# Attention and feed-forward on one core: two block loads moved ahead of waiting copies on GpSimd, and a new order of steps

## The chip, the core and the metric

The kernel runs on one core of a Trainium2 chip. Its engines are TensorE (PE, matrix products; PEld is its weight load), VectorE (DVE), ScalarE (ACT), GpSimd (POOL) and SyncE (SP, which only issues transfers). Each engine works through its own queue in order; semaphores make one engine wait for another. DMA transfers are issued from the queues of SP, ACT and POOL. The metric is the device time of one execution in microseconds (us); lower is better.

## What is computed

Sliding-window causal attention over 8 batch entries, 8 heads, 576 positions, 64 values per head, then a feed-forward layer over all 4608 tokens:

```python
scores = scale * np.matmul(q, k.transpose(0, 1, 3, 2))
rel = pos[:, None] - pos[None, :]
mask = (rel >= 0) & (rel < 64)
scores = np.where(mask, scores, -1000000000.0)
attn = np.exp(scores - max); attn = attn / attn.sum
x = (attn @ v).transpose(0, 2, 1, 3).reshape(4608, 512)
h = x @ w_in                                  # 512 x 2048
out = (h * sigmoid(1.702 * h)) @ w_out        # 2048 x 512
```

All arrays are float32 outside; the kernel computes products in bfloat16.

## The kernel before, in words

**Attention.** Tokens are taken in 36 groups m of 128, that is two query blocks of 64; a batch entry has nine such blocks, so a group can span two entries. A query block j needs the keys of positions 64(j-1) to 64(j+1). Keys and queries must stand transposed (`qt`, `kt`, two sets used in turn by even and odd entries). `scores(m)` (L319) multiplies them into the bank pair psS, `exp` (L335) runs on ACT, `mask` (L339) multiplies by the band on VectorE, `pv` or `pv_two` (L347) multiplies by the values (from `v_nat` for odd j, from `v_off`, the same values shifted by 64 rows, for even j), `norm` or `norm_two` (L363, L365, L391, L392) divides on VectorE, and the result is transposed into `xT`, up to m = 15 by TensorE and an ACT copy (`x_mm`, L415, L424, L434, L431), from m = 16 by a transposing DMA on SP (`x_dma`, L437).

**How rows arrive.** Entries 0 and 1 are loaded in float32 and cast. Of entry 2, the third one, blocks 0 to 2 (128 rows each) are loaded in float32 by SP (`load_qk` L108, `load_v` L87) and cast by GpSimd: the queries and keys of block 2 by the copies L969 and L972, the values by `cast_v` (L101), in three pieces. From block 3 of entry 2 on, `load_bf16(b, i)` (L228, L229) issues three transfers from the GpSimd queue (queries, keys, values) that convert on the way. `turn_dma(b, i)` (L240) then transposes the queries and keys of a block by two DMAs from the SP queue, and `shift_v` (L233, L235) makes the shifted values on GpSimd.

**Feed-forward.** A unit s of `w_in` work is eight or sixteen products into one of two banks psH (`up_mm`, L453), 0.87 us on TensorE. It ends either in one ACT operation (`up_gelu`, L484) or in a tanh on ACT (`up_th`, L464) and a multiplication on VectorE (`up_g`, L479); either frees the bank. Sixteen units make the 512 tokens of a chunk. The product with `w_out` and, for the last chunk, the one with `w_in` are done with seven block products in place of eight (Strassen's way): sums of blocks of g are formed on VectorE (`add_g`, L544), differences of weight blocks once (`add_w`, L528), and the products p1 to p7 (`product`, L568) of each 256 tokens go in two bank chains of psO, which has two banks. `keep_chain` copies a chain's state out in the middle (L113), `add_out` (L593) and `last_of_chain` (L113) write the output tile `o_sb`, of which there are five, and `store` (L584) sends it off, from SP or ACT.

**What sets the order.** The program runs under a manual schedule: every engine executes in the order in which the program issues. Up to L1020 the order is written out as calls. After it a string `plan` holds 727 steps, executed one by one. A step is a letter with numbers:

- `u`s`.g` or `u`s`.t`: unit s, with gelu on ACT, or with tanh and a later `g`s on VectorE
- `c`m scores (`.h`: in two psH banks), `x`m exp (with a load of the ACT table where the last operation was gelu), `m`m mask, `v`m the product with the values, `n`m norm, `t`m transposition
- `l`b.i `load_bf16`, `y`b.i `turn_dma`, `h`b.i `shift_v`
- `p`q.n product n of the 256 tokens q, `a`q.n a sum of g, `w`n.part a difference of weights, `k`q.n.E `keep_chain` on engine E, `o`q.n `add_out`, `z`q.E `last_of_chain`, `s`q.t `store`
- `F K O G X W`: the same for the last chunk's product with `w_in`

As each engine's queue is in order, a step's place in the plan fixes what stands ahead of it on its engine, but an engine runs ahead of the others until it has to wait.

Of the kernel before, what the change touches and what calls it, by code (L numbers as in the profile page):

```python
# [29 lines left out]
def kernel(  # L30
# [39 lines left out]
    def size(i):  # L70
        return P if i < 4 else 64
# [627 lines left out]
    def warm(n):  # L699
# [270 lines left out]
    load_v(2, 2)  # L970
    cast_v(2, 1, parts=(0,))
    nc.gpsimd.tensor_copy(out=rows[0][1][0:size(2), 2, :], in_=stage_of_qk(2, 2)[0:size(2), 1, 0:DM])  # L972
# [15 lines left out]
    load_bf16(2, 3)  # L988
# [20 lines left out]
    load_bf16(2, 4)  # L1009
# [15 lines left out]
        u32.t g32 u33.t g33 l3.0 c10 x10 m10 l3.1 y2.3 v9 h2.3 h2.4 y3.0 h3.0 p2.1 u34.t y2.4 l3.2  # L1025
        c11 n9 x11 g34 u35.t m11 g35 t9 p2.2 v10 w3.0 u36.g n10 l3.3 u37.t g37 u38.g t10 u39.g u40.g
        u41.g u42.g u43.g u44.g u45.g w1.1 u46.g w2.1 l3.4 a2.3 a2.1 w1.0 a2.2 a2.4 h3.1 y3.1 k2.1.V
        w3.1 w2.0 o2.2 a3.3 p2.6 p2.5 h3.2 a3.1 k2.6.V p2.7 k2.7.A w4.1 w4.0 l4.0 y3.2 u47.g y3.3
        a3.2 a3.4 c12 x12 p2.4 o2.5 p2.3 z2.V p3.1 o2.3 h3.3 k3.1.V m12 p3.2 o3.2 h3.4 c13 x13 p3.6
        k3.6.A p3.5 p3.7 m13 y3.4 k3.7.V o3.5 v12 c14 p3.4 z3.A x14 n12 p3.3 t12 p4.1 c15 x15 y4.0  # L1030
        a4.3 a4.1 a4.2 o3.3 a4.4 u48.t u49.g p4.2 u50.g g48 l4.1 y4.1 u51.g u52.g u53.g k4.1.V o4.2
        m15 s2.0 s3.0 m14 c16 x16 v14 n14 m16 c17.h x17 l4.2 p4.5 p4.6 k4.6.V t14 m17 u54.g p4.7 v16
        n16 c18 l4.3 t16 h4.0 l4.4 u55.g u56.g u57.g u58.g k4.7.V o4.5 u59.t g59 u60.g p4.3 o4.3
        a5.3 h4.1 a5.1 s3.1 l5.0 y4.2 h4.2 p4.4 z4.V x18 p5.1 h5.0 l5.3 l5.2 k5.1.A u61.t a5.2 h4.3
        h4.4 y4.3 p5.2 c19 g61 y4.4 p5.6 x19 u62.g u63.g m18 k5.6.V p5.7 k5.7.A m19 v18 o5.2 u64.g
        n18 u65.g l5.1 y5.0 u66.g u67.g h5.1 h5.2 u68.g u69.g p5.5 c20 x20 a5.4 c21.h x21 s4.0 p5.4
# [24 lines left out]
        O33.3 a16.3.0 G33.3 F34.2 p14.2 O34.2 G34.2 K35.1.V u127.g p14.4 o14.2 F35.6 K35.6.A F35.2
        F34.6 K34.6.A a16.1.0 a15.3 F34.5 F35.7 O35.2 G35.2 s12.0 a15.1 p14.5 a16.2.0 z14.A o14.5
# [116 lines left out]
```

The softmax here doesn't subtract the row's maximum and nothing guards it: scores larger than these inputs give would overflow.

## Time and profile before

Six runs gave 293.54 to 300.89 us, median 296.1. The profiled execution took 296.88 us; its span, from the first to the last recorded instruction, was 295.2 us, so 1.7 us lie around it.

| from the profile | us |
| --- | --- |
| profiled execution, own time | 296.88 |
| its span | 295.2 |
| last product of TensorE ends | 291.88 |
| ACT table loads after 70 us, 21 | 26.9 |
| GpSimd issues of `load_bf16`, 81 | 69.8 |
| landing of `kt` transposes, shortest / median / longest | 2.3 / 5.9 / 8.8 |
| landing of `xT` transposes | 2.4 / 5.2 / 8.4 |
| landing of a 256 KB output store from SP, from ACT (median) | 4.2, 2.1 |
| granted TensorE clock | 0.998 |

How to read it: a row of the timeline has start, duration, engine, line, operation, output and inputs, and in brackets the time that the engine stood idle before and what ended that wait. The releaser is inferred and can name the wrong one of several. Matmul ends are modelled, and products overlap slightly, so consecutive products start 0.87 us apart though one row says 1.04. Of the DMA rows, the duration is that of issuing alone; landing comes later.

### The profile page before, as it was taken

What the parts mean: (1) busy time and instruction counts of PE and PEld (TensorE: products, weight loads), DVE (VectorE), ACT (ScalarE), POOL (GpSimd) and SP (SyncE); (2) the same over time, 40 slices, a digit from 0 to 9 for tenths busy, and PEclk for the clock granted to TensorE, in tenths of its full rate; (3) what the DMA queues carried; (4) which work ended last, traced back from release to release, by engine and by line L of the source; (5) the groups of instructions that cost most, each with busy time, mean ns of one, the idle gap of its engine ahead of it and who ended that gap; (6) DMA issues with size and microseconds to landing.
All of it is one profiled execution on the core that took longest, in us unless ns stands there. A gap on an engine that the chain in (4) does not pass through costs nothing.

```text
span 295.2 us, 8971 instructions
## 1 busy us (share of the span) xinstructions
PE 283.9 (96%) x3778; PEld 250.9 (85%) x3783; DVE 196.7 (67%) x377; ACT 181.1 (61%) x289; POOL 137.6 (47%) x191
## 2 busy tenths in 40 slices
PE   8699999999999989999999999999999999999995
PEld 8478455999898878889898999899899899989984
DVE  4667725898998685375546663775887874768771
ACT  3577535877774388776768665776758653456411
POOL 1580446744999989706829876209640000000000
PEclk9999999999999999999999999999999999999999
DMA  7999999996999999999999999999975171001133
GB/s 233 215 205 215 243 240 234 252 153 127 86 132 108 138 145 139 177 169 132 130 184 125 153 137 215 150 179 165 157 82 126 26 192 39 0 2 71 73 124 126
DMA packets 149768, 42.79 MB, mean 145 GB/s; under 512 B 135136, under 2 KB 144864, under 8 KB 149728
## 3 DMA queue, kind: packets, MB, share of 16 engines
q0 software_dynamic: 77712, 13.64, 67.2%
q1 hardware_dynamic: 68208, 25.18, 50.3%
q10 hardware_dynamic: 3808, 3.41, 3.7%
q8 instruction: 29, 0.48, 0.7%
q14 instruction: 11, 0.09, 0.1%
HBM read 36.70 MB, written 9.44 MB: 156 GB/s over the span
## 4 chain that ended last, share of the span: by engine, by line
PE 78%; DMA 9%; POOL 5%; DVE 3%; issue 2%; ACT 2%; SPq 0%; ACTq 0%; DVEq 0%
PE hps L453 32%; PE chain L568 16%; PE part L568 13%; PE ops L491 5%; PE up L668 4%; PE Tacc L347 3%; DMA kt<-rows_k 3%; DMA stage_qk<-in_k_dram 3%; DMA out_dram<-o_sb 3%; PE S L319 3%; POOL v_off L101 2%; DVE stage_qk L528 1%; POOL v_nat L101 1%; POOL w_in_sb L247 1%; PE turn L196 1%
## 5 line engine op out<-in xcount | busy, mean ns | idle before, releaser
L453 PEld LDWEIGHTS <-w_in_sb 128*128 128x128 bf16 x1312 | 109.6, 113 | 4.9 <-issue 0.7
L484 ACT ACTIVATE gT<-hps 128x512 bf16<-128x512 f32 x82 | 48.6, 597 | 34.7 <-PE hps L453 34.4
L453 PE MATMUL hps<-xT_pe,w_in_sb 128*128 128x128 bf16 (+2 forms) x800 | 60.9, 234 | 0.1
L453 PE MATMUL hps<-xT_dma,w_in_sb 128*128 128x256 bf16 x512 | 60.6, 273 | 0.3 <-ACT gT L694 0.3
L568 PEld LDWEIGHTS <-gT 128*128 128x128 bf16 x512 | 49.0, 98 | 5.9
L479 DVE SCALAR_TENSOR_TENSOR gT<-th,hps 128x512 bf16<-128x512 bf16 x46 | 30.8, 684 | 12.4 <-ACT th L464 12.3
L233 POOL COPY v_off<-v_nat 64x528 bf16<-64x528 bf16 x27 | 18.7, 695 | 37.4 <-DMA v_nat<-in_v_dram 36.7
L464 ACT ACTIVATE th<-hps 128x512 bf16<-128x512 f32 x46 | 27.0, 599 | 12.9 <-PE hps L453 12.5
L593 DVE TENSOR_TENSOR o_sb<-part,stage_v 128x256 f32<-128x256 f32 x48 | 20.2, 422 | 21.6 <-PE part L568 12.8
L335 ACT ACTIVATE PT<-S 128x1024 bf16<-128x1024 f32 x28 | 28.5, 1017 | 8.6 <-PE S L319 8.3
L339 DVE TENSOR_TENSOR PT<-PT,band_all 128x1024 bf16<-128x1024 bf16 x32 | 23.7, 750 | 5.4 <-ACT PT L335 5.3
L229 POOL DMA_DIRECT2D v_nat<-in_v_dram x27 | 23.4, 866 | 2.3 <-DMA rows_q<-in_q_dram 1.1
L228 POOL DMA_DIRECT2D rows_k<-in_k_dram x27 | 23.3, 863 | 2.3 <-DMA v_nat<-in_v_dram 2.3
L228 POOL DMA_DIRECT2D rows_q<-in_q_dram x27 | 23.1, 854 | 0.0
L568 PEld LDWEIGHTS <-sums 128*128 128x128 bf16 x192 | 18.6, 98 | 3.7 <-issue 1.6
L568 PEld LDWEIGHTS <-stage_v 128*128 128x128 bf16 x192 | 18.6, 98 | 2.1
L113 ACT COPY stage_v<-chain 128x256 f32<-128x256 f32 x22 | 8.2, 373 | 18.8 <-PE chain L568 18.8
L113 DVE COPY stage_v<-chain 128x256 f32<-128x256 f32 x26 | 10.9, 420 | 11.7 <-PE chain L568 11.5
L392 DVE TENSOR_TENSOR xs<-Tacc,rc 128x128 bf16<-128x128 f32 (+1 forms) x26 | 18.0, 692 | 0.9
L568 PE MATMUL chain<-stage_qk,sums 128*128 128x256 bf16 x128 | 16.6, 272 | 0.4 <-DVE stage_v L113 0.4
L319 PEld LDWEIGHTS <-kt 64*128 64x128 bf16 x576 | 10.4, 95 | 7.4 <-issue 5.2
L568 PE MATMUL chain<-stage_qk,gT 128*128 128x256 bf16 x128 | 16.6, 273 | 0.0
(127 smaller groups left out, 458.4 us busy)
## 6 DMA issues: line engine op xcount, KB each, us to landing
out_dram<-o_sb SPq DMA_DIRECT2D x24, 256.0 KB, 4.2
rows_q<-in_q_dram POOLq DMA_DIRECT2D x21, 128.0 KB, 6.9
rows_k<-in_k_dram POOLq DMA_DIRECT2D x21, 128.0 KB, 7.4
v_nat<-in_v_dram POOLq DMA_DIRECT2D x21, 128.0 KB, 8.1
out_dram<-o_sb ACTq DMA_DIRECT2D x10, 256.0 KB, 2.1
stage_v<-in_v_dram SPq DMA_DIRECT2D x9, 256.0 KB, 7.0
stage_qk<-in_q_dram SPq DMA_DIRECT2D x4, 512.0 KB, 7.3
stage_qk<-in_k_dram SPq DMA_DIRECT2D x4, 512.0 KB, 8.0
```

The costliest lines, as they stand in the source:

```text
L113: (nc.scalar.copy if engine is nc.scalar else engine.tensor_copy)(**kw)
L228: nc.gpsimd.dma_start(out=heads(row_block(b, i, w)), in_=rows_of(src, b, i))
L229: nc.gpsimd.dma_start(out=v_nat[b % 2][0 : size(i), i, :, 0:D], in_=rows_of(v, b, i))
L319: nc.tensor.matmul(st[h % 2][:, t * 256 + hp * 64 : t * 256 + hp * 64 + 64], lhsT=src[1][part, hp, 64 * j : 64 * j + 128], rhs=src[0][part ...
L335: nc.scalar.activation(out=e[:], in_=st[:], func=AF.Exp, scale=scale)
L339: nc.vector.tensor_tensor(out=pt, in0=pt, in1=band_all[:], op=ALU.mult)
L453: nc.tensor.matmul(ps[:, g, :], lhsT=w_in[:, c, (f + g) % 4 : 512 : 4], rhs=xT[ch][:, m0 : m0 + nt // P, c, :], start=(c == 0), stop=(c == 3),
L464: nc.scalar.activation(out=th[:], in_=ps[:], func=AF.Tanh, scale=1.702)
L479: nc.vector.scalar_tensor_tensor(out=g_of(*unit), in0=th[:], scalar=1.0, in1=ps[:], op0=ALU.add, op1=ALU.mult,)
L484: nc.scalar.activation(out=g_of(*unit), in_=ps[:], func=AF.Gelu_apprx_sigmoid, scale=2.0)
L568: nc.tensor.matmul(out[:, :], lhsT=left[:, j], rhs=right[:, j], start=new and j == 0, stop=j == 7, skip_group_check=True,)
L593: nc.vector.tensor_tensor(out=out_half(c, pr, t, half), in0=C_of[c, pr][:], in1=kept(c, pr, at), op=ALU.add)
```

## The change

In the part written out as calls, `load_bf16(2, 3)` and `load_bf16(2, 4)` move up. The first now stands between the copies of block 2's queries and of its keys, the second right after the copy of the keys; that copy moves ahead of `cast_v(2, 1, parts=(0,))`. Before, the first stood behind the key copy and four casts, the second behind three casts more.

The plan is replaced by another one of 730 steps. The same products, sums, loads, transposes and stores are in it. Seventeen of its units instead of fourteen are done by tanh and VectorE. In its first part the differences w1 and w2 stand at the front, scores 12 come right after unit 36 and not after unit 47, and the loads of entries 3 and 4 stand earlier. Stores 4.1, 5.0 and 8.1 stand later and store 7.0 earlier. The last steps are in another order: `p16.4` is now the last product instead of `p17.4`.

The diff, the plan cut to its beginning and end:

```diff
@@ -968,8 +968,10 @@
     up_g(*UU['1.12.128'])
     nc.gpsimd.tensor_copy(out=rows[0][0][0:size(2), 2, :], in_=stage_of_qk(2, 2)[0:size(2), 0, 0:DM])
     load_v(2, 2)
+    load_bf16(2, 3)
+    nc.gpsimd.tensor_copy(out=rows[0][1][0:size(2), 2, :], in_=stage_of_qk(2, 2)[0:size(2), 1, 0:DM])
+    load_bf16(2, 4)
     cast_v(2, 1, parts=(0,))
-    nc.gpsimd.tensor_copy(out=rows[0][1][0:size(2), 2, :], in_=stage_of_qk(2, 2)[0:size(2), 1, 0:DM])
     cast_v(2, 2, parts=(0,))
     cast_v(2, 1, parts=(1,))
     cast_v(2, 1, parts=(2,))
@@ -985,7 +987,6 @@
     UU['1.4.256'] = up_th(*UU['1.4.256'])
     cast_v(1, 3, nc.vector, parts=(1,))
     up_g(*UU['1.4.256'])
-    load_bf16(2, 3)
     turn_dma(2, 2)
     UU['1.8.256'] = up_mm(1, 8, 4, 256, 128, wide=True)
     x_mm(7, psT, "T")
@@ -1006,7 +1007,6 @@
     UU['1.4.384'] = up_th(*UU['1.4.384'])
     up_g(*UU['1.12.256'])
     up_g(*UU['1.4.384'])
-    load_bf16(2, 4)
     UU['1.8.384'] = up_mm(1, 8, 4, 384, 128, wide=True)
     UU['1.8.384'] = up_th(*UU['1.8.384'])
     up_g(*UU['1.8.384'])
@@ -1022,51 +1022,51 @@
 
 
     plan = """
-        u32.t g32 u33.t g33 l3.0 c10 x10 m10 l3.1 y2.3 v9 h2.3 h2.4 y3.0 h3.0 p2.1 u34.t y2.4 l3.2
-        c11 n9 x11 g34 u35.t m11 g35 t9 p2.2 v10 w3.0 u36.g n10 l3.3 u37.t g37 u38.g t10 u39.g u40.g
-        u41.g u42.g u43.g u44.g u45.g w1.1 u46.g w2.1 l3.4 a2.3 a2.1 w1.0 a2.2 a2.4 h3.1 y3.1 k2.1.V
-        w3.1 w2.0 o2.2 a3.3 p2.6 p2.5 h3.2 a3.1 k2.6.V p2.7 k2.7.A w4.1 w4.0 l4.0 y3.2 u47.g y3.3
-        a3.2 a3.4 c12 x12 p2.4 o2.5 p2.3 z2.V p3.1 o2.3 h3.3 k3.1.V m12 p3.2 o3.2 h3.4 c13 x13 p3.6
-        k3.6.A p3.5 p3.7 m13 y3.4 k3.7.V o3.5 v12 c14 p3.4 z3.A x14 n12 p3.3 t12 p4.1 c15 x15 y4.0
-        a4.3 a4.1 a4.2 o3.3 a4.4 u48.t u49.g p4.2 u50.g g48 l4.1 y4.1 u51.g u52.g u53.g k4.1.V o4.2
-        m15 s2.0 s3.0 m14 c16 x16 v14 n14 m16 c17.h x17 l4.2 p4.5 p4.6 k4.6.V t14 m17 u54.g p4.7 v16
...
-        p16.5 a17.4.1 o17.2 k16.7.V o16.5 p17.5 s15.1 p16.4 o17.5 s17.1.1 s17.0.0 p17.3 o17.3
-        s17.0.1 z16.A s16.1 p16.3 o16.3 s16.0 p17.4 z17.A s17.1.0
+        u32.t g32 w1.0 w2.0 c10 p2.1 l3.0 l3.1 w1.1 l3.2 x10 v9 y2.3 l3.3 n9 h2.3 h2.4 u33.t g33
+        u34.t g34 y2.4 m10 c11 x11 p2.2 l3.4 y3.0 k2.1.A t9 u35.t m11 u36.t h3.0 c12 g35 h3.1 x12
+        g36 v10 y3.1 n10 l4.1 u37.g u38.t l4.0 t10 u39.g g38 h3.2 y3.2 u40.g u41.g u42.g u43.g w3.0
+        w2.1 u44.g u45.g h3.3 w3.1 u46.g a2.3 y3.3 o2.2 a3.3 a3.1 h3.4 a2.1 a2.2 w4.0 p2.6 k2.6.A
+        p2.5 m12 p2.7 a3.2 w4.1 a2.4 k2.7.V c13 x13 p2.4 o2.5 m13 z2.V p2.3 p3.1 v12 c14 y3.4 k3.1.A
+        a4.3 a4.1 p3.6 k3.6.A o2.3 n12 p3.2 t12 l4.2 p3.7 x14 u47.t u48.t l4.4 a3.4 o3.2 c15 x15
+        h4.0 k3.7.V y4.0 p3.5 p3.4 g47 z3.A m14 m15 y4.1 u49.t g48 a4.2 p4.1 k4.1.V c16 o3.5 v14
+        p4.6 x16 n14 k4.6.A h4.1 c17 x17 p3.3 o3.3 u50.g s3.1 t14 y4.4 l4.3 p4.2 o4.2 p4.7 u51.g
+        p4.5 g49 l5.0 u52.g a4.4 h4.2 k4.7.V p4.4 m17 m16 v16 n16 u53.g c18 s3.0 u54.g l5.2 u55.g
+        u56.g a5.3 u57.g a5.1 u58.g u59.g u60.t o4.5 p4.3 h4.3 h4.4 a5.2 z4.V g60 x18 t16 o4.3 p5.1
+        k5.1.V l5.3 y4.2 s2.1 u61.t h5.0 p5.2 s2.0 p5.6 k5.6.V c19 x19 m18 y4.3 y5.0 g61 o5.2 u62.g
+        p5.7 s4.0 a5.4 a6.3 u63.t p5.5 l5.1 h5.1 u64.g u65.g u66.g u67.g u68.g u69.g g63 c20 l5.4
+        m19 v18 a6.1 y5.2 k5.7.V p5.4 a6.2 a6.4 n18 u70.g u71.g o5.5 z5.V p6.1 k6.1.V l6.0 p5.3 o5.3
+        x20 a7.3 m20 p6.6 k6.6.A p6.2 o6.2 t18 c21 x21 p6.7 h5.2 y5.1 p6.5 h5.3 h5.4 c22 m21 y5.3
+        v20 x22 k6.7.V p6.4 n20 y5.4 u72.g u73.g u74.g t20 a7.1 u75.g u76.g u77.g z6.V y6.0 p7.1
+        a7.2 m22 o6.5 p6.3 o6.3 c23.h k7.1.V x23 c24 x24 h6.0 s5.1 p7.2 p7.6 m23 v22 s6.0 n22 u78.g
+        u79.g u80.g u81.g u82.g u83.g u84.g a7.4 k7.6.V p7.7 t22 l6.1 y6.1 o7.2 p7.5 m24 l6.2 y6.2
+        c25.h x25 h6.1 c26 k7.7.V o7.5 p7.4 x26 z7.A m25 h6.2 u85.g s7.1 p7.3 v24 p8.1 m26 n24 t24
+        s6.1 u86.g u87.g u88.g l7.0 k8.1.V u89.g l6.3 u90.g u91.g u92.g u93.g u94.g l7.1 o7.3 a9.3
+        a9.1 a8.3 y6.3 a8.1 a8.2 u95.g h6.3 p8.6 k8.6.V p8.2 c27.h x27 p8.7 s7.0 a9.2 h7.0 y7.0 o8.2
+        p8.5 k8.7.A l6.4 c28 h6.4 y7.1 x28 c29.h x29 h7.1 a8.4 p8.4 z8.A o8.5 p8.3 m27 v26 o8.3
+        u96.g p9.1 k9.1.A u97.g a9.4 s8.0 n26 p9.6 l7.3 p9.2 l7.2 h7.2 m28 h7.3 l7.4 h7.4 k9.6.A
+        u98.t g98 u99.g p9.7 k9.7.A y6.4 u100.g u101.g a10.3 a10.1 a10.2 p9.4 m29 u102.g u103.g t26
+        z9.V p10.1 a10.4 o9.2 p9.5 k10.1.V p10.6 o9.5 s9.1 y7.2 c30.h x30 k10.6.V m30 c31 p9.3 o9.3
...
+        p15.3 G34.3 a17.3.1 a17.1.1 o15.3 a17.1.0 z15.A p16.1 a17.2.0 s15.1 a17.2.1 a17.4.0 p17.1
+        p17.2 a16.4.0 k16.1.V k17.1.A p17.6 a16.4.1 p16.2 a17.4.1 o16.2 s14.0 k17.6.A o17.2 p17.7
+        s15.0 p16.6 k16.6.V k17.7.A p17.5 p17.4 p16.7 p16.5 z17.V s17.0.0 o17.5 k16.7.V o16.5 p17.3
+        p16.3 s14.1 s17.1.0 p16.4 o16.3 s16.0 o17.3 s17.1.1 z16.A s16.1 s17.0.1
```

## The prediction

> **What bounds the kernel now.** I read first the busy totals, then the busy time of each engine by stretches, then the list of who waited for whom, with TensorE alone.
>
> ```profile
> PE 283.9 (96%) x3778; PEld 250.9 (85%) x3783; DVE 196.7 (67%) x377; ACT 181.1 (61%) x289; POOL 137.6 (47%) x191
> ```
>
> ```profile
> 60.00:80.00 20.00, 19.65 (x420) 18.39 (x418) 18.35 (x34) 15.45 (x26) 11.12 (x17) 1.00 1.04 117
> 80.00:90.00 10.00, 9.93 (x176) 9.80 (x174) 9.32 (x15) 7.06 (x13) 9.84 (x12) 1.00 1.95 128
> 90.00:100.00 10.00, 9.57 (x120) 8.26 (x119) 7.65 (x14) 5.20 (x8) 9.54 (x13) 1.00 1.63 114
> 100.00:110.00 10.00, 8.98 (x135) 7.77 (x134) 7.66 (x16) 5.49 (x8) 8.73 (x11) 1.00 2.46 144
> 120.00:130.00 10.00, 9.14 (x85) 8.65 (x83) 4.89 (x9) 6.74 (x12) 4.56 (x7) 1.00 1.90 191
> 280.00:296.00 16.00, 11.88 (x109) 10.40 (x107) 7.37 (x20) 1.86 (x5) 0.00 (x0) 0.94 0.31 115
> ```
>
> Columns: stretch, length, then busy us of PE, PEld, DVE, ACT, POOL, then the granted clock. TensorE sets the time at full clock. Summed over the stretches from 60 to 280 us it is idle 3.26 us, 2.7 of that in the five stretches shown before the last. The change alters no matmul and nothing that runs before about 66 us. So the most that the reordering can bring there is 3.26 us, 1.1% of 296.9, and only if it adds no wait. What the idle time waited for:
>
> ```profile
> PE S L319 <- DMA kt<-rows_k: 0.9, 1, 0.9
> PE part L568 <- DVE o_sb L593: 0.9, 1, 0.9
> PE chain L568 <- DVE stage_v L113: 0.4, 1, 0.4
> PE Tacc L347 <- POOL v_off L101: 0.3, 1, 0.3
> ```
>
> In order of time: v10 waits 0.35 for a GpSimd cast (78.5 us), p2.7 waits 0.42 for k2.6 on VectorE (92.0), c15 waits 0.94 for the transposed keys of y3.2 (106.5), p4.3 waits 0.85 because o4.5 had no free output buffer until store s2.0 or s3.0 landed (126.0). The first two belong to compute queues, the last two are single late transfers. Short waits of 0.33 and 0.12 lie later.
>
> **Part 1, the GpSimd loads.** The timeline of POOL:
>
> ```profile
> 65.36 0.70 POOL L969 CAST rows_q<-stage_qk 128x512 bf16<-128x512 f32 x1 [2.61 <-DMA stage_qk<-in_q_dram]
> 70.52 0.61 POOL L101 CAST v_off<-stage_v 64x512 bf16<-64x512 f32 x1 [4.47 <-PE pxt L415]
> 71.19 0.61 POOL L972 CAST rows_k<-stage_qk 128x512 bf16<-128x512 f32 x1
> 74.12 0.90 POOL L228 DMA_DIRECT2D rows_q<-in_q_dram  x1
> 78.98 0.70 POOL L228 DMA_DIRECT2D rows_q<-in_q_dram  x1
> 81.01 0.92 POOL L228 DMA_DIRECT2D rows_q<-in_q_dram  x1
> ```
>
> The 4.47 us before 70.52 ended with stage_v landing (PE is named, but the cast reads only stage_v, loaded from 66.85 on). The change fills this hole: from 66.05 three issues of load (2,3) at 0.88 each (74.12 to 76.8: 2.65 us) to 68.7, the key copy at 69.3 instead of 71.8, three issues of load (2,4) at 0.70 to 71.4. The casts behind them start at 71.4 instead of 70.5; those four took 3.0 and the next three 2.2, so they end at 76.6 instead of 79.0, and l3.0 begins at 76.6 instead of 81.0. So GpSimd is 4.4 us ahead, v10's 0.35 goes, and every later load can start earlier. On SP, y2.2's key transpose, at 71.83 before, has its rows 2.5 us earlier, and y2.3 no longer waits until 77.6. The cost is nothing as long as v10, which needs the last of the seven casts, comes after 76.6; it comes near 80. If the two v loads, now beside six loads more, landed 3 us later than before, that cover is used up.
>
> **Part 2, the start of the new plan.** It puts three more weight differences on VectorE (w1.0, w2.0, w1.1) ahead of n9, g33 and g34. The rows of VectorE there:
>
> ```profile
> 72.03 0.99 DVE L339 TENSOR_TENSOR PT<-PT,band_all 128x1024 bf16<-128x1024 bf16 x1 [0.77 <-ACT PT L335]
> 72.95 1.87 DVE L479 SCALAR_TENSOR_TENSOR gT<-th,hps 128x512 bf16<-128x512 bf16 x3
> 75.57 0.69 DVE L365 TENSOR_TENSOR xs<-Tacc,rc 128x512 bf16<-128x512 f32 x1
> 78.51 1.07 DVE L528 TENSOR_TENSOR stage_qk<-w_out_sb 128x1024 bf16<-128x1024 bf16 x1
> ```
>
> The difference operation appears at 0.69 (82.41) and at 1.07, the long one beside GpSimd casts; the eight average 0.80. In the new plan the three lie beside GpSimd casts (71.4 to 76.6). Walk: m9 72.03 to 72.95, two g at 0.62 to 74.2, three w at 0.80 to 76.6, n9 (0.92, as 75.34 to 76.26) to 77.5; bounds 77.2 and 78.3 with w at 0.69 and 1.07. TensorE has the same sum of work before t9 in both plans (p2.2 takes u35's place, 0.87 each) and transposed at 76.92. So t9 waits 0.3 to 1.4, taken 0.6. Then u35 needs the bank that g33 frees, 0.62 behind n9: it starts at 78.2 (77.9 to 79.0). Behind g33 stand g34, m10, m11, g35, so the bank for v10 comes free at about 80.8; v10, n10 (1.70, as 79.50 to 81.26) and t10 follow at 83.45. Before, t10 ran at 81.87; with c12 (0.34), new ahead of it, 82.2 is the equal point. Cost +1.25, bounds +0.9 and +2.0, the removed 0.35 already in it.
>
> The row bears on port sharing: the mask took 0.99 beside casts, 0.68 at 74.74 beside DMA issues. The Trainium skill, "SBUF — State Buffer", section "Who interferes with whom", says that a two-input VectorE operation in SBUF and a reading GpSimd one exclude each other for a whole instruction. By that rule each of the three could wait for a whole cast (0.61) and n9 would end at 79.0, a wait of 2.1 instead of 0.6; the rows seen stayed below that.
>
> From t10 to p3.1 the old 0.42 goes (k2.6 moves to ACT, with p2.5 as cover). But k2.7 (VectorE, 0.42) is now read by p2.4 with only c13 (0.34) between: about 0.3. And p3.1 needs the bank that z2 frees, behind m13, which waits for x13 and c13: 0.6 to the start of the exponential (as 73.07 to 73.67), 1.02, 0.7 and 0.4 make 2.75 against 2.1 of TensorE work; 0.65, of which the 0.3 is already spent. Net +0.2; bounds -0.4 and +0.9.
>
> **Part 3, the later steps.** The key transposes took 2.3 to 8.8 us to land, median 5.9. The late one:
>
> ```profile
> 97.66 1.21 SPq L240 DMA_TRANSPOSE kt<-rows_k  x1
> ```
>
> It was issued 7.6 us before c15 wanted it (105.29). In the new order l3.2 is issued from 81.9, its keys land by 90 (7.4 median from 82.8), y3.2 goes out near 91.4, and c15 comes at about 103.5: 12 us, above the longest landing seen. The same sum gives 8.7 for c13 and 11 to 13 for c14, c16, c17, c18; before, c13, c14 and c17 had 7.4 to 7.8. The 0.94 goes. For o4.5 the stores move apart: s3.1 now stands ahead of s3.0 and t16 on SP, some 13 us before p4.3 against a longest store landing of 8.4; the 0.85 goes. Sum -1.8; bounds 0 and -2.25. Stores held back (s4.1, s5.0, s8.1) each hold one of five output buffers longer; at every first write one is still free, and the nearest store is more than 3 us older. One thinner place: v18 comes 6.4 us later, so t18's last transpose would land 5.2 (median) after 144.6, at 149.8, and u72 wants it near 151; at the longest landing, 8.4, it waits 2. I take 0.3 for all such new waits after 97 us, near the two short late ones of before (0.33 and 0.12); bounds 0 and 2. The ends of TensorE's chains move to ACT (z, two more) and the table loads, counted in the plan by changes between exp and gelu, fall from 21 to 19: 2.6 us of ACT, which is idle over a third of the time and hides it: nothing.
>
> **Part 4, the end.** Before, the last product ended at 291.88, and behind it:
>
> ```profile
> 291.93 0.37 ACT L113 COPY o_sb<-chain 128x256 f32<-128x256 f32 x1 [2.27 <-PE chain L568]
> 292.33 0.34 ACTq L584 DMA_DIRECT2D out_dram<-o_sb  x1
> ```
>
> That last store is 128 KB; in the new plan s16.1 is last on ACT, 256 KB (2.1 us against 1.8), with s16.0 issued just before on the same queue and s17.0.1 on SP. +0.3; bounds 0 and +0.9.
>
> **Sum.** On the profiled execution: 296.88 + 1.25 + 0.2 - 1.8 + 0.3 + 0.3 = 297.1. It lies 0.8 above the median of six runs (296.1), which I take off: 296.3.
>
> **Rivals.** (a) Slower: VectorE's queue decides. If w and a operations take 1.07 to 1.12 throughout, because GpSimd is now never idle beside them, part 2 costs +2.0 and +0.9; with the late waits of part 3 at +2, the end at +0.9 and only the 0.94 regained, 296.1 + 4.9 = 301.0; with late waits at half, 300. It decides when n9 ends after 78 us. For: VectorE was busy 18.35 of 20 us there already. Against: 0.80 is the mean of those eight rows. (b) Faster: all 3.26 us of idle go and the walk's waits do not come, because VectorE runs w at 0.6 apart: 296.1 - 3.26 + 0.3 = 293.1. For: the new margins. Against: the structural chain to p3.1. (c) The loads do not come earlier in effect: transposes stay behind each other on SP and 0.94 stays; 297.2, still no change.
>
> **Chances.** The forecast with (c) 0.47, (a) 0.40, (b) 0.13. A difference under 1% (3 us) is about what a measurement of this kernel cannot tell from none. Range 293.2 to 300.4: from (b)'s end to (a) with part of its waits. The likeliest case alone spans 294.5 to 298.
>
> **What would show it.** Load (2,3) issued near 66 us and l3.0 near 77; t9 or u35 waiting for VectorE between 77 and 79; no wait of S on kt and none on o_sb between 100 and 130; t10 near 83.4; 3.3 to 3.9 us from the last product to the end. If TensorE idles under 1.5 us from 60 to 280, (b) is right; over 5 us, (a).

## The result, and the profile after

The changed kernel takes 298.98 us (median of 21 runs, 296.43 to 301.43), beside 295.87 us for the kernel before (42 runs, 293.37 to 302.91). The ratio is 1.0098, interval 1.0072 to 1.0124, so it is about 1% slower. (The ratio leaves out runs more than 1.5% above the fastest of the same kernel.)

The profiled execution shows none of that: 296.68 us against 296.88. The profile therefore has two things to answer: which stalls went and came, and why the usual run is 2.3 us longer than this one. The busy totals and the stretches of the kernel after, with the columns of before:

```profile
PE 282.9 (96%) x3778; PEld 250.0 (85%) x3783; DVE 195.6 (66%) x378; ACT 179.0 (61%) x288; POOL 138.8 (47%) x191
```

```profile
60.00:80.00 20.00, 18.45 (x378) 17.11 (x376) 18.27 (x31) 14.13 (x25) 14.27 (x20) 1.00 1.41 142
80.00:90.00 10.00, 9.56 (x198) 9.20 (x196) 8.67 (x15) 8.06 (x14) 9.86 (x13) 1.00 2.23 117
90.00:100.00 10.00, 8.09 (x133) 6.94 (x132) 9.79 (x17) 4.77 (x8) 9.83 (x12) 1.00 1.96 141
100.00:110.00 10.00, 10.00 (x168) 8.92 (x162) 6.77 (x14) 5.83 (x10) 9.72 (x15) 1.00 2.86 140
120.00:130.00 10.00, 10.00 (x106) 9.52 (x104) 5.14 (x9) 6.95 (x11) 9.80 (x12) 1.00 1.96 169
280.00:296.00 16.00, 11.15 (x103) 9.74 (x100) 6.14 (x17) 1.49 (x4) 0.00 (x0) 0.91 0.32 116
```

From 100 to 280 us TensorE is never idle; before, 2.41 us were lost there. In exchange 1.55 us are lost from 60 to 80, 0.44 from 80 to 90 and 1.91 from 90 to 100, where before lost 0.35, 0.07 and 0.43. The sum from 60 to 280 us rises from 3.26 to 3.90. The waits themselves, in TensorE's timeline of after:

```profile
76.87 0.41 PE L319 MATMUL S<-qt,kt 64*128 64x64 bf16 x16 [1.55 <-DMA kt<-rows_k]
80.78 0.22 PE L347 MATMUL Tacc<-v_off,PT 128*64 128x65 bf16 x1 [0.18 <-DVE gT L479]
81.67 1.95 PE L453 MATMUL hps<-xT_pe,w_in_sb 128*128 128x128 bf16 x32 [0.19 <-DVE gT L479]
96.51 1.03 PE L568 MATMUL chain<-stage_qk,gT 128*128 128x256 bf16 x8 [1.91 <-DVE stage_v L113]
```

The first is c11, which waits for the keys of y2.2; the last is p2.4, which waits for k2.7.

**Why y2.2 is late.** GpSimd's and SP's timelines of after, the transposes of y2.2 last:

```profile
64.28 0.61 POOL L969 CAST rows_q<-stage_qk 128x512 bf16<-128x512 f32 x1 [2.46 <-DMA stage_qk<-in_q_dram]
64.84 0.90 POOL L228 DMA_DIRECT2D rows_q<-in_q_dram  x1
...
67.47 0.64 POOL L972 CAST rows_k<-stage_qk 128x512 bf16<-128x512 f32 x1
...
72.53 0.61 POOL L101 CAST v_off<-stage_v 64x512 bf16<-64x512 f32 x1 [1.60 <-DMA stage_v<-in_v_dram]
...
77.37 0.89 POOL L228 DMA_DIRECT2D rows_q<-in_q_dram  x1
```

```profile
66.76 2.74 SPq L240 DMA_TRANSPOSE qt<-rows_q  x1
69.61 1.22 SPq L240 DMA_TRANSPOSE kt<-rows_k  x1
```

The loads start at 64.84 and l3.0 at 77.37, 3.6 us before the 81.01 of before (the whole start of this execution is 0.54 us earlier). The key transpose is issued at 69.61, 2.2 us earlier than before (71.83). Its rows were ready 3.7 us earlier (the copy ends at 68.11, before at 71.80), but the issue of the queries' transpose took SP 2.74 us; before, 1.64. The data land only when c11 begins, 7.2 us after the issue. Before, they landed in 2.4 us, and c11 started without a wait. The same two rows in before, SP's and TensorE's:

```profile
71.83 1.19 SPq L240 DMA_TRANSPOSE kt<-rows_k  x1
```

```profile
75.66 0.41 PE L319 MATMUL S<-qt,kt 64*128 64x64 bf16 x16
```

The transfers from 60 to 84 us, a view with the queue's share of the 16 DMA engines and the median us from issue to landing, first of after and then of before:

```profile
q0 software_dynamic: 8926, 1.12, 74.9%
...
stage_v<-in_v_dram SPq DMA_DIRECT2D x2, 256.0 KB, 5.8
...
qt<-rows_q SPq DMA_TRANSPOSE x5, 6.2
```

```profile
q0 software_dynamic: 5549, 0.70, 46.3%
...
stage_v<-in_v_dram SPq DMA_DIRECT2D x2, 256.0 KB, 3.7
...
qt<-rows_q SPq DMA_TRANSPOSE x3, 3.7
```

The queue of the GpSimd loads takes 75% of the engines' time instead of 46%. By these medians the value loads land 2.1 us later and the queries' transposes 2.5 us later (five against three of them); the key transposes took 4.8 instead of 3.6 us, and the float32 loads of queries and keys, sent ahead of the moved loads, took about as long as before (3.5 and 5.3 against 3.8 and 5.2).

The landing of this one transpose, y2.2's keys, separates the kernels of this document: 2.4 us in before and in `e2_plan_only`, whose loads stand at the old places, 6.1 to 7.7 us in all ten profiles in which a moved load is issued ahead of it, 3.9 and 4.4 us in `e11_old_mended` and `e12_new_mended`, where the transpose is issued first and a load follows. The view of the transfers issued at that time, of before, after and `e11_old_mended`:

```profile
kt<-rows_k SPq DMA_TRANSPOSE x1, 2.4
```

```profile
kt<-rows_k SPq DMA_TRANSPOSE x1, 7.2
```

```profile
kt<-rows_k SPq DMA_TRANSPOSE x1, 3.9
```

That the loads delay it is so shown; that they do it by their share of the DMA engines is argued from the queue's share, and no run tries it alone.

**Why p2.4 waits.** VectorE's timeline of after:

```profile
92.96 1.10 DVE L544 TENSOR_TENSOR stage_v<-gT 128x1024 bf16<-128x1024 bf16 x1
93.99 1.11 DVE L528 TENSOR_TENSOR stage_qk<-w_out_sb,stage_qk 128x1024 bf16<-128x1024 bf16 x1
95.02 1.10 DVE L544 TENSOR_TENSOR sums<-gT,sums 128x1024 bf16<-128x1024 bf16 x1
96.05 0.41 DVE L113 COPY stage_v<-chain 128x256 f32<-128x256 f32 x1
```

VectorE has work without a gap and is behind. The sums and weight differences take 1.10 where the same kinds of operation take 0.68 at other times (86.10, 86.70 and 97.92 us), and k2.7, the last row, stands behind them. From 92.83 to 96.6 us GpSimd runs its shift copies, so the two engines work in SBUF at once. That the copies make the operations longer was not tried by a run of its own; one difference (91.33 us) takes 1.10 beside load issues alone.

**The end.** In ACT's timeline of after, 3.85 us pass from the last product (ending at 291.15) to the end of the span at 295.0; before, 3.3:

```profile
291.20 0.37 ACT L113 COPY o_sb<-chain 128x256 f32<-128x256 f32 x1 [6.63 <-PE chain L568]
291.61 0.34 ACTq L584 DMA_DIRECT2D out_dram<-o_sb  x1
```

The small total difference is made up so: idle time +0.64, end +0.55, the part up to 60 us -0.54, and the same 3778 matmuls recorded as busy 1.0 us less (283.9 to 282.9). Sum -0.35, measured -0.20. What makes the recorded busy time shorter, the program's order of groups or the modelled ends, was not tried.

**The usual run.** Each run lists its mean granted clock. Of the 22 runs listed for after, the profiled one among them, 8 have 0.997 or more (median 296.9 us) and 14 have 0.991 to 0.994 (median 299.2 us). The profiled one is one of the eight. A mean of 0.994 over 296 us is 1.8 us lost. The kernel before has a mean under 0.997 in 22 of 94 runs; its other 72 have a median of 295.9 us. So about 1 us of the 3.1 between the two medians is there at full clock too, and the rest goes with the larger share of runs at a lowered clock.

### The profile page after: what moved, and what is told of

The parts are those of the page before. It is cut to its first block, busy times and chain, and to the rows that moved or that the text cites. A ratio compares the mean times of both kernels' runs of the same rounds, so it can differ in the third digit from the quotient of the medians.

```text
span 295.0 us, 8970 instructions
## 1 busy us (share of the span) xinstructions
PE 282.9 (96%) x3778; PEld 250.0 (85%) x3783; DVE 195.6 (66%) x378; ACT 179.0 (61%) x288; POOL 138.8 (47%) x191
## 4 chain that ended last, share of the span: by engine, by line
PE 80%; DMA 9%; POOL 4%; DVE 2%; ACT 1%; issue 1%; SPq 1%; DVEq 0%; POOLq 0%; ACTq 0%
PE hps L453 32%; PE chain L568 19%; PE part L568 14%; PE up L668 4%; PE ops L491 4%; PE Tacc L347 3%; DMA stage_qk<-in_q_dram 3%; PE S L319 3%; DMA stage_v<-in_v_dram 3%; DMA kt<-rows_k 2%; DMA stage_qk<-in_k_dram 2%; POOL v_off L101 1%; POOL v_nat L101 1%; SPq L240 1%; PE turn L196 0%
## 5 line engine op out<-in xcount | busy, mean ns | idle before, releaser
L484 ACT ACTIVATE gT<-hps 128x512 bf16<-128x512 f32 x79 | 47.1, 598 | 37.3 <-PE hps L453 37.1
L453 PE MATMUL hps<-xT_dma,w_in_sb 128*128 128x256 bf16 x512 | 59.9, 273 | 0.0
L479 DVE SCALAR_TENSOR_TENSOR gT<-th,hps 128x512 bf16<-128x512 bf16 x49 | 32.8, 683 | 18.1 <-ACT th L464 18.0
L464 ACT ACTIVATE th<-hps 128x512 bf16<-128x512 f32 x49 | 28.8, 599 | 12.9 <-PE hps L453 12.3
L339 DVE TENSOR_TENSOR PT<-PT,band_all 128x1024 bf16<-128x1024 bf16 x32 | 22.7, 714 | 8.0 <-ACT PT L335 5.1
```

Source lines behind the costliest of these rows:

```text
L339: nc.vector.tensor_tensor(out=pt, in0=pt, in1=band_all[:], op=ALU.mult)
L453: nc.tensor.matmul(ps[:, g, :], lhsT=w_in[:, c, (f + g) % 4 : 512 : 4], rhs=xT[ch][:, m0 : m0 + nt // P, c, :], start=(c == 0), stop=(c == 3),
L464: nc.scalar.activation(out=th[:], in_=ps[:], func=AF.Tanh, scale=1.702)
L479: nc.vector.scalar_tensor_tensor(out=g_of(*unit), in0=th[:], scalar=1.0, in1=ps[:], op0=ALU.add, op1=ALU.mult,)
L484: nc.scalar.activation(out=g_of(*unit), in_=ps[:], func=AF.Gelu_apprx_sigmoid, scale=2.0)
```

## The experiments

Each ratio is to the kernel before, whose median beside these kernels was 295.6 to 296.5 us.

Theory A: the loads moved up delay y2.2's transposes. Theory B: VectorE's order around k2.7 makes p2.4 wait. Theory C: the clock that falls behind such waits makes the usual run longer than the profiled one; its rival D is that the clock falls somewhere unrelated, at the start or the end of the span.

**Each half alone.** `e1_loads_only` is after with the plan of before; `e2_plan_only` is before with the plan of after.

```diff
 # e1_loads_only
+    load_bf16(2, 3)
+    nc.gpsimd.tensor_copy(out=rows[0][1][0:size(2), 2, :], in_=stage_of_qk(2, 2)[0:size(2), 1, 0:DM])
+    load_bf16(2, 4)
     cast_v(2, 1, parts=(0,))
 # e2_plan_only
-        u32.t g32 u33.t g33 l3.0 c10 x10 m10 l3.1 y2.3 v9 h2.3 h2.4 y3.0 h3.0 p2.1 u34.t y2.4 l3.2
...
+        u32.t g32 w1.0 w2.0 c10 p2.1 l3.0 l3.1 w1.1 l3.2 x10 v9 y2.3 l3.3 n9 h2.3 h2.4 u33.t g33
...
```

> Old plan, only the two loads moved up. Theory A (the moved loads delay the transposes of y2.2): the key transpose of y2.2, issued near 69.6 us instead of 71.8, takes about 7 us to land instead of under 3.8, and c11 waits 1 to 2 us for it; v10's wait for the GpSimd cast (0.35) is gone; ratio to before 1.002 to 1.006. Rival B (the loads are free, the new plan alone costs): c11 does not wait, ratio 0.998 to 1.000.

Measured: 297.67 us, ratio 1.0068 [1.0044, 1.0091]. TensorE's timeline and then its granted clock (the third number from the end) in stretches of 4 us behind that wait:

```profile
77.85 0.41 PE L319 MATMUL S<-qt,kt 64*128 64x64 bf16 x16 [2.93 <-DMA kt<-rows_k]
```

```profile
78.00:82.00 4.00, 4.00 (x75) 3.17 (x70) 2.34 (x5) 3.37 (x4) 4.00 (x6) 0.67 0.83 60
82.00:86.00 4.00, 3.93 (x70) 3.76 (x65) 2.28 (x5) 1.86 (x4) 3.84 (x6) 0.90 2.02 131
```

Theory A holds: the loads without the new plan make the same wait, and the kernel is 0.68% slower than before. The clock lacks 0.33 and 0.10 of 4 us, 1.72 us together, which is 3.4 us at half.

> New plan, the two loads at their old places. Theory A: c11 does not wait for y2.2, but c12, now right after u36 (near 79 us), waits for the keys of y2.3, whose load is issued only at 74 to 77 us and whose transposes landed after 82: a wait of 3 to 6 us, ratio to before 1.010 to 1.020. Rival B: the plan costs the same as the whole change, ratio 1.008 to 1.012, with the wait of p2.4 for k2.7 (1.9 us) as the largest.

Measured: 303.45 us, ratio 1.027 [1.0221, 1.032], more than expected. The new plan asks for block 3's keys at c12, before the old loads have brought them:

```profile
86.08 0.61 PE L319 MATMUL S<-qt,kt 64*128 64x64 bf16 x16 [7.03 <-DMA kt<-rows_k]
```

The wait began at 79.05. The clock is at half from 82.8 to 89.6 us, 6.8 us, so it fell within the wait and about half of the stretch lies behind it; all six runs have a lowered mean. c11 does not wait here. So the two halves belong together: the plan needs the loads early, and the loads make it wait elsewhere.

**The same kernel again.** No edit; to catch a usual run in a profile.

> The changed kernel once more, for a second profile. Of its 22 runs so far 9 had a mean granted clock of 0.997 to 1.0 and took 296.4 to 297.8 us, 13 had 0.991 to 0.994 and took 297.9 to 301.4. Theory C (a wait of TensorE near 94 us or near 75 us, of about 2 us or more, lets the granted clock fall for a stretch): a profile at 0.993 shows a stretch of lower clock right behind one of these two waits. Rival D (the clock falls somewhere unrelated, at the start or the end of the span): the stretch lies before 60 or after 280 us. Ratio to before 1.007 to 1.013 by both.

Measured: 298.88 us, ratio 1.011 [1.0067, 1.0153]; the profiled run 298.12 us. (Of the 22 runs before it, 8 and 14 had the two clocks, not 9 and 13.) Its waits are those of the first profile, 1.61 at c11 and 1.91 at p2.4, and behind the second this stands in the stretches:

```profile
92.00:96.00 4.00, 2.28 (x34) 1.88 (x33) 4.00 (x6) 2.88 (x4) 3.83 (x5) 1.00 2.12 140
96.00:100.00 4.00, 3.80 (x20) 2.78 (x20) 3.26 (x7) 0.00 (x0) 4.00 (x6) 0.57 1.76 93
100.00:104.00 4.00, 4.00 (x81) 3.45 (x80) 2.83 (x6) 0.79 (x3) 3.78 (x6) 1.00 2.15 157
```

From 96 to 100 us TensorE is busy for 3.80 us, but its clock is 0.57: 3.4 us at half speed, 1.7 us lost. The difference between the two profiled runs is 1.44 us. Theory C holds for this execution; `e8_both_c11` below shows one of D's kind, so D is not excluded for the others. The Trainium skill, "TensorE: Matmul & The Clock Gate", Part 1, has the clock fall to half after an idle window of about 3.4 us and counts in windows of 3413 ns. The length of the slow stretch agrees; the idle time ahead of it does not, since a wait of 1.91 us stands there.

**VectorE's order.**

```diff
 # e4_k27_act
-        p2.7 a3.2 w4.1 a2.4 k2.7.V c13 x13 p2.4
+        p2.7 a3.2 w4.1 a2.4 k2.7.A c13 x13 p2.4
 # e6_sums_later
-        y3.3 o2.2 a3.3 a3.1 h3.4
+        y3.3 o2.2 h3.4
...
-        p2.7 a3.2 w4.1 a2.4 k2.7.V c13 x13 p2.4 o2.5 m13 z2.V p2.3
+        p2.7 w4.1 a2.4 k2.7.V c13 x13 p2.4 o2.5 m13 z2.V a3.1 a3.2 a3.3 p2.3
 # e10_sums_apart
+        z2.V a3.3 a3.1 a3.2 p2.3
...
-        k3.1.A a4.3 a4.1 p3.6 k3.6.A o2.3 n12 p3.2
+        k3.1.A p3.6 k3.6.A o2.3 n12 a4.3 a4.1 p3.2
```

(In `e6_sums_later`, `e7_both` and `e8_both_c11` the in-place sum a3.1 comes ahead of a3.3, so a3.3 subtracts the summed block and these three do not compute the layer's output; the number and sizes of the operations are the same.)

> The changed kernel with keep_chain 2.7 on ACT instead of VectorE. Theory E (the 1.9 us wait before p2.4 is VectorE's queue): p2.4 then waits only for w4.1, which stands two operations earlier; its wait falls from 1.9 to 0.6 to 1.0 us, part of it comes back before p3.1 (bank of z2 behind m13); net gain 0.5 to 1.3 us. If theory C holds as well, the lower clock becomes rarer and the ratio to before falls to 0.998 to 1.004; if not, it stays at 1.004 to 1.008.

Measured: 299.25 us, ratio 1.0113 [1.0074, 1.0151]; no gain. The 1.91 breaks up into 0.17, 0.71 and 0.70: o2.5 still stands behind the same sums on VectorE and p2.3 waits for it, and z2 stands behind m13, which itself waited 0.70 for the exponential. c11's 1.55 stays, and 7 of 10 runs have a lowered mean. Not k2.7's engine but VectorE's backlog and its order are the cause.

> The changed kernel with a3.1, a3.2 and a3.3 moved behind z2 on VectorE. Theory E (VectorE's queue makes the 1.9 us before p2.4): the queue before k2.7 is 2.1 to 3 us shorter, p2.4 waits 0.2 to 0.5, p3.1 0.3 to 0.7 (z2 behind m13); net gain 0.9 to 1.4 us and, because the wait is under 1 us, no lower clock right behind it. Ratio to before 1.003 to 1.007; the rest is c11. Rival G (VectorE is late anyway and the sums are missed later): p3.6 or p3.7 waits 1 us or more and the ratio stays at 1.008 to 1.012.

Measured: 297.49 us, ratio 1.0031 [0.9991, 1.007]. The wait at p2.4 is 0.23, but two new ones appear, p3.2 behind o2.3 and t12 behind n12:

```profile
94.54 1.03 PE L568 MATMUL chain<-stage_qk,gT 128*128 128x256 bf16 x8 [0.23 <-DVE stage_v L113]
100.17 1.03 PE L568 MATMUL part<-w_out_sb,gT 128*128 128x256 bf16 x8 [0.71 <-DVE o_sb L593]
101.86 0.62 PE L424 MATMUL pxt<-ident,xs 128*128 128x128 bf16 x8 [0.65 <-DVE xs L392]
```

Theory E holds for p2.4, and rival G's waits at p3.6 and p3.7 do not come. The ratio is at the low end of what was expected; c11 still waits 1.54, and 6 of 12 runs have a lowered mean.

> After, with a3.3, a3.1, a3.2 moved behind z2 and a4.3, a4.1 moved behind n12, all on VectorE. If VectorE's order around k2.7 and o2.3 is the cause of the waits from 94 to 102 us, p2.4 waits about 0.2 instead of 1.9, p3.2 and t12 (0.71 and 0.65 in e6_sums_later) under 0.3 each, the profiled run takes about 295.5 and the ratio is 0.998 to 1.002, with the 1.55 at c11 left. Rival: the clock that falls behind c11's wait is what is left of the loss; then the runs at a granted clock under 0.997 stay at half or more and the ratio stays at 1.003 as in e6_sums_later.

Measured: 297.5 us, ratio 1.007 [1.0036, 1.0104]. In the profile nothing waits on VectorE from 98 us on and p2.4 waits 0.23, as the first theory said; but c11 waited 2.30 us in this execution, the clock fell behind it (0.58 from 78 to 82 us), and 6 of 10 runs have a lowered mean. The rival names what was left, though its ratio of 1.003 was too low. Theory B is right on the waits. What mending them is worth stays open: the interval overlaps that of after (1.0072 to 1.0124), and the four runs at full clock have a median of 296.9 us, as in after.

**The loads' place.**

```diff
 # e5_keys_first (e7_both: e5 and e6 together; e8_both_c11: e7 with c11 x11 behind p2.2)
     load_v(2, 2)
-    load_bf16(2, 3)
     nc.gpsimd.tensor_copy(out=rows[0][1][0:size(2), 2, :], in_=stage_of_qk(2, 2)[0:size(2), 1, 0:DM])
+    load_bf16(2, 3)
     load_bf16(2, 4)
```

> The changed kernel with the copy of block 2's keys ahead of both moved loads. Theory A (the moved loads share the DMA engines with y2.2's transposes; its keys are also released late, behind three issues): the keys' transpose is issued about 2 us earlier and lands 1 to 2 us earlier, c11's wait falls from 1.6 us to 0 to 0.8, c12 does not wait; gain 0.8 to 1.6 us, ratio to before 1.003 to 1.008. Rival F (the landing is set by the loads alone, however early the transpose is issued): c11 still waits 1.3 us or more, ratio as the change, 1.008 to 1.012.

Measured: 299.32 us, ratio 1.0093 [1.006, 1.0126]; the expected gain missed. The keys' transpose is issued only 0.6 us earlier (68.99), because the load of the rows landed later, and it still takes 7.0 us to land. That is what rival F says of the landing. c11's wait falls to 0.63 (the releaser named is ACT, but the weight load of the same product waits for the keys), p2.4's 1.91 stays, and c12, whose keys come from load (2,3), takes over with 0.97:

```profile
80.70 0.41 PE L319 MATMUL S<-qt,kt 64*128 64x64 bf16 x16 [0.97 <-DMA kt<-rows_k]
```

> Both edits of the two kernels before this. If theories A and E hold: TensorE idles under 1.5 us between 60 and 280, the mean granted clock is 0.997 or above in at least 3 of 4 runs, and the time is 294.0 to 295.5, ratio to before 0.994 to 1.000. If the lower clock comes from elsewhere, it stays in half of the runs or more and the ratio is 1.003 or above.

Measured: 297.22 us, ratio 1.0054 [1.0019, 1.0088]. No single wait is above 0.70, but there are eight, 2.9 us together. Four of 12 runs have a lowered mean. The idle time, 3.0 us, and the time miss what was expected; the rival's ratio comes with fewer lowered runs than it said.

> As the kernel before this, and scores 11 one product later (behind p2.2, 0.87 us). If c11 still waits in e7, its wait is up to 0.87 us shorter here, at the price of up to 0.5 us before v10, which needs m11: ratio to before 0.992 to 1.000, equal to or up to 0.3% below e7. If c11 does not wait in e7, this one is 0.2 to 0.5 us slower than e7.

Measured: 297.9 us, ratio 1.0056 [1.0027, 1.0085]. c11 still waits 1.04 and unit 35 now 0.65 for ACT: moving c11 back uncovers what stood behind it. The profiled execution took 298.12 us at a mean clock of 0.994 although no wait from 60 to 280 us is above 1.04. Its low stretch lies at the start of the program, behind a wait for the first rows; TensorE's timeline and the stretches:

```profile
10.28 0.92 PE L146 MATMUL turn<-ident,rows_q 128*128 128x128 bf16 x8 [2.00 <-DVE rows_q L113]
```

```profile
10.00:14.00 4.00, 3.70 (x30) 2.91 (x30) 2.35 (x5) 1.60 (x2) 2.87 (x4) 0.57 1.18 183
14.00:18.00 4.00, 4.00 (x97) 2.51 (x97) 2.27 (x6) 2.97 (x4) 3.72 (x7) 1.00 1.17 191
```

This wait lies in a part that the change does not touch, and its length differs from one execution to the next: 0.97 in after, 1.75 in before, where the clock stayed full. So some of the lowered runs of every kernel, before among them, can come from the start.

**Old plan and new plan, each mended.**

```diff
 # e11_old_mended, from before
     nc.gpsimd.tensor_copy(out=rows[0][0][0:size(2), 2, :], in_=stage_of_qk(2, 2)[0:size(2), 0, 0:DM])
+    nc.gpsimd.tensor_copy(out=rows[0][1][0:size(2), 2, :], in_=stage_of_qk(2, 2)[0:size(2), 1, 0:DM])
     load_v(2, 2)
     cast_v(2, 1, parts=(0,))
-    nc.gpsimd.tensor_copy(out=rows[0][1][0:size(2), 2, :], in_=stage_of_qk(2, 2)[0:size(2), 1, 0:DM])
+    load_bf16(2, 3)
...
     up_g(*UU['1.4.256'])
-    load_bf16(2, 3)
     turn_dma(2, 2)
...
-        k2.6.V
+        k2.6.A
...
-        y3.4 k3.7.V
+        y3.4 s2.0 k3.7.V
 # e12_new_mended: the GpSimd order of e11, load (2,4) where load (2,3) stood before, e10's plan, and
-        c12 g35 h3.1 x12 g36 v10 y3.1 n10 l4.1
+        g35 h3.1 g36 v10 y3.1 n10 c12 x12 l4.1
```

> Before, with its old plan, but the key copy of block 2 right behind its query copy, load (2,3) behind the first cast of v (about 71 us instead of 74.1), k2.6 on ScalarE and store s2.0 moved up behind y3.4. If the hole on GpSimd can be used without delaying y2.2 as long as no load is issued between its copies and its transposes, c11 waits for nothing, v10's 0.35, p2.7's 0.42 and p4.3's 0.85 go, c15's 0.94 stays or halves: idle time 60 to 280 us 1 to 2 us instead of 3.26, ratio 0.993 to 0.998. Rival: whatever is issued early on GpSimd comes back as a late transpose (c11 or c12 over 0.5 us), or the first v10 waits for casts that now stand behind a load; ratio 1.000 to 1.006.

Measured: 295.71 us, ratio 1.0006 [0.9973, 1.0039]. The waits at the start went as the theory said; the ratio did not come. TensorE waits in three places:

```profile
104.07 0.29 PE L319 MATMUL S<-qt,kt 64*128 64x64 bf16 x8 [0.27 <-DMA kt<-rows_k]
147.06 1.04 PE L453 MATMUL hps<-xT_dma,w_in_sb 128*128 128x256 bf16 x8 [1.04 <-DMA xT_dma<-xs]
256.58 1.03 PE L453 MATMUL hps<-xT_dma,w_in_sb 128*128 128x256 bf16 x8 [0.33 <-ACT gT L694]
```

With shorter gaps TensorE idles 1.79 us instead of 3.26. The wait of 1.04 for a transposing DMA of `xT` is new and was not expected. c11 waits for nothing although the load is 3.6 us earlier (70.52): the transposes of y2.2 were issued (67.30 and 69.35) before it, and the keys' landed in 3.9 us. The profiled run took 294.49 us, yet the median is no better than that of before: at full clock 295.6 against 295.9. So 1.5 us less idle time in one profile does not show in the median, whose runs spread over 3 us.

> The new plan of after with e10's order of the sums, the GpSimd order of e11 (key copy of block 2 at once, load (2,3) behind the first cast of v), load (2,4) three casts later, and c12, x12 moved behind n10. If the two large waits of after (1.6 at c11, 1.9 at p2.4) make its loss, directly and by the clock that falls behind them, this run has neither: idle time 60 to 280 us under 1.5, the profiled run 295 to 296, at most a quarter of the runs at a granted clock under 0.997, ratio 0.998 to 1.002. Rival: the new plan needs the rows of block 3 as early as the moved loads brought them; then c12 waits over 1.5 us for keys, the clock falls behind that wait as in e2_plan_only, and the ratio is 1.005 or more. A ratio under 0.997 would say that the new plan, mended, beats the old one; the longer end (about 0.5 us) speaks against that.

Measured: 298.98 us, ratio 1.0079 [1.0045, 1.0114]; neither theory. c11 and c12 wait for nothing, p2.4 waits 0.20, but from 76 to 81 us the waits show that c11's had hidden:

```profile
76.75 0.40 PE L415 MATMUL pxt<-ident,xs 128*128 128x128 bf16 x4 [0.49 <-DVE xs L365]
77.34 1.05 PE L453 MATMUL hps<-xT_pe,w_in_sb 128*128 128x128 bf16 x16 [0.19 <-DVE gT L479]
79.95 1.05 PE L453 MATMUL hps<-xT_pe,w_in_sb 128*128 128x128 bf16 x16 [1.55 <-ACT xT_pe L434]
```

t9 waits 0.49 for n9 on VectorE, a unit 1.55 for t9's copy on ACT, which c12 no longer covers. With 0.44 at 85.24, 0.68 at 112.59 and smaller ones TensorE idles 4.61 us from 60 to 280, more than the 3.90 of after, and 8 of 12 runs have a lowered mean. So the loss at the start of the new plan is not c11's wait alone: with the keys in time the queues of VectorE and ACT end last there.

**The end.** `e9_old_end` is after with its last steps in the old order. In it k16.7 copies the chain after p16.4's addition, so it does not compute the layer's output; the number and sizes of the operations are the same.

```diff
-        p17.5 p17.4 p16.7 p16.5 z17.V s17.0.0 o17.5 k16.7.V o16.5 p17.3
-        p16.3 s14.1 s17.1.0 p16.4 o16.3 s16.0 o17.3 s17.1.1 z16.A s16.1 s17.0.1
+        p17.5 p16.7 p16.5 p16.4 k16.7.V o17.5 s17.1.1 o16.5 z16.A s16.1 p17.3
+        p16.3 s14.1 s17.0.0 o17.3 s17.0.1 o16.3 s16.0 p17.4 z17.A s17.1.0
```

> After, with the last steps put in the order of the plan before: p17.4, z17 and the 128 KB store s17.1.0 come last, s16.1 and s16.0 ahead of them. If the end costs what the size and number of the last stores make it, the time from the last product's end to the end of the span falls from 3.85 us to 3.3, and the ratio from 1.0098 to about 1.008 (bounds 1.006 and 1.010); all waits between 60 and 280 us as in after (1.6 at c11, 1.9 at p2.4). Rival: the 0.5 us lie in how the last products are ordered, not in the stores; then TensorE idles 0.3 or more within the last 10 us and the ratio stays at 1.010.

Measured: 300.93 us, ratio 1.0188 [1.0133, 1.0243]. It missed and settles nothing: the new order put a wait of 0.85 for an output buffer ahead of p17.3, c11 waited 2.72 in this execution, and from the last product to the end it took 4.1 us with the 128 KB store last. Only this follows: a smaller last store alone does not shorten the end. The old plan had 3.3 in all three profiles (before, e1, e11), the new one 3.8 to 4.7 in all ten with its own last steps; why stays open.

**The clock over all kernels.** Between 60 and 280 us the profiles of after, e1 to e6, e9, e10 and e12 show a wait of 1.5 us or more; of their 106 runs 75 have a mean clock under 0.997. The profiles of before, e7, e8 and e11 have none above 1.04 there; of their 130 runs 31 have. This goes together and is no proof for a single run. Only the profiled executions show where the clock fell. c11's wait differs from 1.54 to 2.72 us between executions of kernels that are alike up to it (after, e3, e4, e6, e9, e10), so longer waits are a part of the usual run too, and e9 shows 2.72 and 1.91 with no fall behind either.

## Why the prediction was right in its range, and where it failed

The measured 298.98 lies in the range of 293.2 to 300.4; the forecast of 296.3 is 2.7 below it, and the ratio's interval straddles the 1% between "no change" and "slower". Step by step:

- **Part 1, GpSimd ahead by 4.4 us**: 3.6 us measured at l3.0, 3.1 with the earlier start taken out; l3.0 came at 77.37, forecast near 77. The v loads did land 2.1 us later (5.8 for 3.7), within the 3 us of cover, and v10 no longer waits for a cast. Right in kind, 1.3 us short.
- **Part 1, "y2.2's key transpose has its rows 2.5 us earlier" and the loads cost nothing**: this step failed. The rows were 3.7 us earlier and the transpose's issue 2.2, but the keys landed later: 7.2 us after the issue instead of 2.4, a wait of 1.55 us in after, 2.93 in e1. The step looked at what is queued on GpSimd; beyond issue time it allowed the moved loads only a delay of the v loads, and what they do to the transposes of SP was not priced. Under the old plan e1 gives 0.68% for it, where the whole change gives 0.98%; as each half makes other waits, the two do not simply add up.
- **Part 2, start to t10, +1.25 (0.9 to 2.0)**: t10 at 83.46 was forecast at 83.45, but by another wait. From the same start it is 2.13 us later than before (81.87), 1.8 beyond c12's product: in the bounds. c11's wait hid the waits of t9; e12 shows the forecast 0.6 as 0.49, and 1.55 more on ACT that the walk did not have.
- **Part 2, k2.7 to p2.4, 0.3**: mis-sized, 1.91. From t10 to p3.1 that makes +1.5 for the forecast +0.2, beyond the bound of +0.9. The walk had no backlog on VectorE there; three operations of 1.10 in a row stood ahead of k2.7. The term of rival (a), sums at 1.07 to 1.12 throughout, was the right price here, though not at the start: n9 ended at 77.24, before the 78 from which (a) was to decide. The 0.65 forecast behind z2 and m13 stayed hidden in the longer wait; e4, which takes that away, shows it as 0.70. With 3.90 us of idle time the profile lies between the marks set for (b), 1.5, and (a), 5.
- **Part 3, -1.8 (0 to -2.25), and +0.3 for new waits**: all 2.41 us of idle time after 100 us are gone, c15's and o4.5's waits and the short ones; no new one came, and the feared t18 did not wait. Rival (c) falls with it.
- **Part 4, +0.3 (0 to 0.9)**: 0.55. Inside; its reason, the size of the last store, is not supported by e9.
- **The sum, 297.1 for the profiled execution**: measured 296.68. By the terms as measured, 1.8 + 1.5 - 2.4 + 0.55, it would have been 298.3. That 0.54 for the earlier start and 1.0 of recorded busy time, which the sum did not have, brought it back near the forecast is luck.
- **"Minus 0.8", profiled to median**: this step failed too. It was taken over from before, where the profiled run lies above the median; after, it lies 2.3 below. The prediction priced a wait at its length and had no term for the clock. In e3 the clock falls behind p2.4's 1.91, in e1 and e10 behind c11's 2.93 and 2.30, at about 1.7 us each time. 14 of the 22 runs have a lowered mean, for 22 of 94 before; how many of the 14 owe it to these two waits is not shown, as e8's fell at the start. That the median stayed in the range is owed to the range's upper end, which stood for VectorE's queue alone and had no part for the late transpose or the clock.

## What to carry to other kernels

A load moved into a hole of its queue can delay the transfers beside it: look at which short transfer (here a transpose) is wanted next, and let that be issued first. Price a TensorE wait of about 2 us (the shortest that the clock fell behind here was 1.91) at its length plus, in a part of the runs, 1.7 us for the stretch at half clock, and compare medians and clocks of many runs before believing one profile. When a wait is mended, look up what it had covered: five times here the next one in the queue took its place.

## What the runs showed of the hardware

TensorE's clock fell to half for 3.4 us behind waits of 1.91 us (e3), 2.00 (e8, at the start), 2.30 (e10) and 2.93 (e1), and for 6.8 us from within one of 7.03 us (e2). The fall came 2.1 to 4.4 us after TensorE went idle. Behind 1.55 and 1.91 us in after, and 2.72 and 1.91 in e9, it did not come.

A key transpose that landed in 2.4 us took 6.1 to 7.7 us with converting loads issued ahead of it, and 3.9 to 4.4 with the first of them issued 1.2 us behind it.

VectorE's two-input operations on 128x1024 bf16 values took up to 1.11 us while GpSimd copied in SBUF, and 0.68 away from the copies; the copies took 0.97 there and 0.62 with VectorE idle (103.91 us). It is not so each time: at 146.56 us of after the operation took 0.68 and the copy beside it 1.18, and the 1.10 at 91.33 has no copy beside it. In the main that agrees with the Trainium skill, "SBUF — State Buffer", section "Who interferes with whom", by which a VectorE operation with two inputs in SBUF and a GpSimd operation that reads there shut each other out. The 0.42 more is less than one whole GpSimd copy (0.62).
